# A gated FFT filter and state-space layer on one Trainium2 core: a third buffer for the skip products, and a new order of all five engines

## The chip, the core and the metric

The kernel runs on one NeuronCore of a Trainium2 chip, in one launch. The metric is the device time of one execution in microseconds. Five engines take instructions, each strictly in its own written order: PE (matrix multiplication; its weight loads are shown apart as PEld), DVE (vector), ACT (scalar and activation), POOL, which here mostly issues accumulating DMAs, and SP, which only issues DMAs. They wait for each other through semaphores.

## The reference

`x` is 2048 tokens by 1024 features. Two branches are computed from it and mixed by a gate of one number per token:

```python
g = sigmoid((x * gate_w).sum(-1, keepdims=True))
# A: spectral filter over both axes
a = irfft2(rfft2(x) * (w_r + 1j * w_i))
# B: diagonal complex state-space layer
h[t] = Lam_bar * h[t-1] + B_bar @ x[t]          # 1024 complex states, 2048 steps
b = 2 * (h @ Cmat.T).real + x * Dskip
out = g * a + (1 - g) * b
```

Types in and out are bfloat16.

## The kernel before

Both branches run interleaved from the start to the end, so that PE always has a matmul to do. The work is cut into some 900 pieces, each a generator step of a Python function. The string `ORDER` names one piece per letter, and `PIECES` gives the order of the 169 vector steps of the state-space recurrence (letter `v`). Pieces are issued in that order, and it fixes the order on all five engines; `SLOTS` says which of four PSUM slots (1024 fp32 columns each) each PSUM tile takes. Nothing is rescheduled later, so an instruction that waits holds up everything behind it on its engine.

The stages that the prediction speaks of:

- **Head.** `load_x` brings in `x`; `turn` (L938) transposes it on PE; `turn_out` (L947) and `fold` (L961 to L972) prepare it on DVE; `fd` (L442 to L455) multiplies by the DFT along the features, `fd_out` (L461) moves each result from PSUM on ACT; `s1` (L474) is the first DFT step along the tokens, done as small 64-row matmuls, and `s1_out` (L489) moves it. Between these, ACT and DVE build tables for the recurrence (`sincos`, L1129 to L1136, `make_tab`, L281 to L306). A PSUM slot is free for the next PE piece when its ACT or DVE copy is done.
- **Middle.** `unit_mm` (L410) multiplies `x` by B in eight chunks of 256 tokens, `unit_out` (L420) copies out, and DVE runs the recurrence (L340 to L387) with ACT's help (L372). The spectral branch goes on with `s2` (L609) and `is1` (L648).
- **Output stage.** `early_mm` (L732) multiplies the states by C for ten tiles of 128 tokens, in halves. `scale_y` (L763, ACT) multiplies a half by 1-g into a tile `ye` (two buffers), and `early_store` (L773, SP) stores it in `y_scratch` in DRAM. `mul_skip` (L788, DVE) forms x times Dskip; `scale_skip` (L798, ACT) multiplies a half of it by 1-g into one of two buffers `su`; `add_skip` (L804, POOL) adds the buffer to the stored half in `y_scratch` by an accumulating DMA. So L798 waits until the add of two halves earlier has read its buffer, that is, has landed. Meanwhile `is2` (L681) is the next spectral step, and `is2_out` (L690, ACT) copies its result into `ZT`.
- **End.** `spectral_mm` (L825, L829), `spectral_out` (L836, ACT) and `spectral` (L844 to L865, DVE) finish branch A; `add_late` (L870, POOL) adds `y_scratch` to it, and `close` (L878, SP) stores the tile. Tiles 13 to 15 come last: `own_mm` (L746) fills `ps_q`, `skip_last` (L911, DVE) forms their skip part and `last_out` (L918, DVE) the output.

Of the kernel before, what the change touches and what calls it, by code (L numbers as in the profile page):

```python
# [14 lines left out]
FP32 = mybir.dt.float32  # L15
BF16 = mybir.dt.bfloat16
# [6 lines left out]
K = 512  # L23
H = K // 2
P = 128
# [16 lines left out]
TURN_DVE = tuple(range(16))  # L42
CLOSES = (0, 1, 2, 3, 10, 4, 5, 11, 12, 6, 7, 8, 9)
PIECES = (
# [7 lines left out]
)  # L52
SLOTS = (
    "0123012301230123021302130231023102302302130230123013021302301201320320213023021310102312012301230210",
    "2302021302130230230213132012031203203123120310321032103210130212031203120",
)
MIRROR = (6, 7, 8, 9)
ORDER = (
    "xTxUfTUVfVVa|2xTTGfVVVrrffa|tfUUtGGFFaxEfftffTTxUESbSbtfU2fFTaxAxTffUUfrFAE2fftxSaakFtEAEtfxbbbbbtTT",
    "TFtTbEbUUbFSUUf~ttfFEufSUUU1UbSSArESttfFAAAftFtbbbttEEwttthH~tfthfftufFFSHbtAtttvfvEEtvgvbSASKhtt1r1",  # L60
    "AtAe1vttrtHtr~1vftve111~htuuhttvtFrttF1ttvtHfvthh1vv1tttEttvcEvccccvccctHvSevvSSFcHHwFAAhhEwScKvE11v",
    "KvvSccctttvvtvvAhKvHeevhvcccvv1nAA1KK1swHvvvvvHHsYvvvvkMvvvvssssvhvvvvvHvvnnLYYsvvvvvvnNWssJNsJNNvsh",
    "MhsvsvvJvsvWyHMss344jhvvMM3hHvLvv5vWmm++HnH54v56nMyvvMMWv78378v4nnmmJNvJNvv5hv5vJ56Yvhv4NJyNjYvM+vvM",
    "453WM787HH44y55hH+mm67h8Hv+n7vWm3Nn54JWYvvnvv558468+vvvhMv3vmvJj5NMMv77+8484vYnJN+ydmvyN55JWvvvHhd6h",
    "3H787mM8Hvv555+mjn6M44hYN77vv+5vm3n55HJv644dvyJ8n87N7+Jmv5v5v5vvv+8vh6NnYvym7vv878Hh8qhq+mNviqJivHh+",
    "miiiIqIniv+vHHvIIvvYyivvIJXv+IvvqvYvvnIqviXNvyiJnimqiIinmvYNIiihIIIvvvvvvvJvvNNvq%iiIIIIv++hHHlzlvpp",
    "hvllzZZPZZZZPRRQQRRRmXvHdJhRpzzDmD+ZZRZZHvPZZlJQvoRpOvQvPlDzBzZZovZvOlZpovRYRZlZDzzvvoRRBDoOOvoyQRQB",
    "BlvDDv+POBZOZRBZZvZvlZzzpvZZQDoovvQoDCZYZZooZ9PooYRyRRRDyYRRQQ9CC9000999DDD09000",
)

EVEN = ((0, 0), (2, 1), (2, 0), (0, 1))
# [73 lines left out]
def kernel(  # L145
# [50 lines left out]
    fx = ctx.enter_context(tc.tile_pool(name="fx", bufs=1, side="right"))  # L196
# [8 lines left out]
    def psum(shape, name, dtype=FP32):  # L205
        return ps.tile(shape, dtype, name=name, tag=next(slots, "ps"), bufs=1 if SLOTS else 4)
# [27 lines left out]
    fft = {}  # L234
# [190 lines left out]
                        recur(c, slice(0, 8), lambda c=c: xQ[:, 2 * (c % 2):2 * (c % 2) + 2].rearrange("p e (r j) t -> p e r (j t)", r=2).rearrange("p e r (j t) -> p e r j t", t=TS))  # L425
                    yield

    Acol = fx.tile([P, 2, 16], BF16, name="Acol")
    t1_w = turn1_dram.rearrange("(g j) m k -> j m g k", g=2)
    A1s, X1s, psf, pss = {}, {}, {}, {}  # L430

# [101 lines left out]
    def middle():  # L533
        after_ia()
        yield
        JP_sb, KRS_sb, Wc = fft["JP"], fft["KRS"], fft["Wc"]

        def reverse_m(src_bf, ncol, name):
            rps = psum([P, 16, ncol], name + "_ps")
            nc.tensor.matmul(rps[:, 0, :], lhsT=JP_sb[:, 1, :], rhs=src_bf[:, 0, :], start=True, stop=True)  # L540
            nc.tensor.matmul(rps[:, 1:16, :], lhsT=JP_sb[:, 0, :], rhs=src_bf[:, 15:0:-1, :], start=True, stop=True)
            return rps

        wrps = reverse_m(Wc, 4, "Wrev")
        yield
        Wrev = fx.tile([P, 16, 4], FP32, name="Wrev")
        nc.scalar.copy(out=Wrev, in_=wrps)
        yield
        Wh = fx.tile([P, 16, 4], FP32, name="Wh")
        nc.gpsimd.tensor_add(out=Wh[:, :, 0:4:2], in0=Wc[:, :, 0:4:2], in1=Wrev[:, :, 0:4:2])  # L550
        nc.gpsimd.tensor_sub(out=Wh[:, :, 1:4:2], in0=Wc[:, :, 1:4:2], in1=Wrev[:, :, 1:4:2])
        AB = fx.tile([P, 2, 2, 16], FP32, name="AB")
        Wq = Wh.rearrange("p b (c r) -> p c r b", r=2)
        nc.gpsimd.tensor_add(out=AB[:, 0], in0=Wq[:, 0], in1=Wq[:, 1])
        nc.gpsimd.tensor_sub(out=AB[:, 1], in0=Wq[:, 0], in1=Wq[:, 1])
        nc.gpsimd.tensor_scalar_mul(out=AB, in0=AB, scalar1=0.25)
        yield
        aps = psum([32, P], "aps", BF16)
        nc.tensor.transpose(out=aps, in_=Acol.rearrange("p g j -> p (g j)"), identity=ident)
        yield  # L560
        Bcol = fx.tile([32, 3, 4, 16], BF16, name="Bcol")
        nc.scalar.copy(out=Bcol[:, 0:2], in_=aps.rearrange("j (r b a) -> j r a b", r=2, a=4))
        nc.scalar.activation(out=Bcol[:, 2], in_=Bcol[:, 0], func=ACT.Copy, scale=-1.0)
        yield
        zps = psum([P, 2, 16], "zps")
        Kc_sb, Ks_sb = fft["K3"][:, 0], fft["K3"][:, 1]
        for i in range(8):
            nc.tensor.matmul(zps, lhsT=(Kc_sb, Ks_sb)[i // 4][:, i % 4, :], rhs=Bcol[:, i // 4:i // 4 + 2, i % 4, :],
                             start=(i == 0), stop=(i == 7))
        yield  # L570
        Zp = fx.tile([P, 16, 2], BF16, name="Zp")
        nc.scalar.copy(out=Zp, in_=zps.rearrange("p c b -> p b c"))
        yield
        zrp = reverse_m(Zp, 2, "Zrev")
        yield
        Zr = fx.tile([P, 2, 16], FP32, name="Zr")
        nc.scalar.activation(out=Zr[:, 1], in_=zrp[:, :, 1], func=ACT.Copy, scale=-1.0)
        yield
        Q = fx.tile([P, 2, 2, 2, 16], FP32, name="Q")
        each = lambda t: t.unsqueeze(2).to_broadcast([P, 2, 2, 16])  # L580
        every = lambda t: t.unsqueeze(1).to_broadcast([P, 2, 2, 16])
        nc.scalar.copy(out=Zr[:, 0], in_=zrp[:, :, 0])
        yield
        nc.vector.tensor_mul(out=Q[:, 0], in0=each(AB[:, 0]), in1=every(Zp.rearrange("p b r -> p r b")))
        yield
        nc.vector.tensor_mul(out=Q[:, 1], in0=each(AB[:, 1]), in1=every(Zr))
        nc.vector.tensor_add(out=Q[:, 0], in0=Q[:, 0], in1=Q[:, 1])
        yield
        Qb = fx.tile([P, 16, 2], BF16, name="Qb")
        nc.vector.tensor_sub(out=Qb[:, :, 0], in0=Q[:, 0, 0, 0], in1=Q[:, 0, 1, 1])  # L590
        nc.vector.tensor_add(out=Qb[:, :, 1], in0=Q[:, 0, 1, 0], in1=Q[:, 0, 0, 1])
        yield
        qps = psum([P, 32], "qps")
        nc.tensor.matmul(qps, lhsT=KRS_sb[:, 2, :], rhs=Qb.rearrange("p b r -> p (b r)"), start=True, stop=True)
        yield
        Qn = fft["Qn"] = fx.tile([P, 16, 2], BF16, name="Qn")
        nc.scalar.copy(out=Qn.rearrange("p b r -> p (b r)"), in_=qps)
        yield
# [186 lines left out]
    def mul_skip():  # L785
        for tb in range(16):
            if tb not in DIAG:
                nc.vector.tensor_mul(out=xs[tb], in0=xs[tb], in1=fft["Db"])  # L788
                yield

    xgs = {}

    def scale_skip():
        xg = up.tile([P, 2, 2, K], BF16, name="su")
        for tb in range(NEARLY):
            for hf in range(2):
                xgs[tb, hf] = xg[:, hf].rearrange("p a k -> p (a k)").bitcast(FP32)
                nc.scalar.activation(out=xgs[tb, hf], in_=xs[tb][:, K * hf:K * (hf + 1)], func=ACT.Copy, scale=omg[:, tb:tb + 1])  # L798
                yield

# [237 lines left out]

    gB = cpool.tile([P, 16], FP32, name="gB")
    omg = cpool.tile([P, 16], FP32, name="omg")  # L1040
    fft["JP"] = fx.tile([P, 2, P], BF16, name="JP_sb")
    fft["KRS"] = fx.tile([P, 3, P], BF16, name="KRS_sb")

    def load_turns():
# [140 lines left out]
    def once(f):  # L1185
        f()
        yield
# [8 lines left out]
        "%": once(load_Gi), "Y": load_skip(), "y": mul_skip(), "m": scale_skip(), "+": add_skip(), "d": make_dgD(), "X": turn_own(),  # L1196
        "l": spectral_mm(late_tiles), "z": spectral_out(late_tiles), "Z": spectral(late_tiles), "Q": add_late(), "D": close(),
        "p": spectral_mm(own_tiles), "P": spectral_out(own_tiles), "R": spectral(own_tiles), "o": own_mm(), "O": own_out(), "B": own_add(),
# [40 lines left out]
```

## Time and profile before

| | us |
|---|---|
| median of 3 runs | 301.17 (300.79 to 302.21) |
| profiled execution | 303.33 |
| its span, first to last instruction | 301.6 |
| PE busy | 292.6 |
| DVE busy | 284.2 |
| ACT busy | 209.5 |
| POOL busy | 81.0 |

The span is what the profile's time axis shows; the profiled execution's own time is 1.7 us longer. PE's granted clock is 1.00 of full speed throughout. PE has 2446 matmuls, DVE 359 instructions, ACT 323. In rows of the profile, `x16` counts instructions merged into one row, `<-` leads from what is written to what is read, and a bracket or a trailing `<-` names what ended an engine's idle time.

### The profile page before, as it was taken

The page shows a single profiled execution, that of the slowest core. Times are in us where ns is not written, and L with a number is a line of the kernel's source. Part 1 is how long each engine was busy: PE and PEld are TensorE (multiplying, and loading weights), DVE is VectorE, ACT ScalarE, POOL GpSimd, SP SyncE. Part 2 cuts the span into 40 slices and gives each one's busy share as a digit, 9 for nine tenths or more (in the row PEclk, how much of TensorE's full clock was granted, in tenths as well). Part 3 has the DMA queues.
Part 4 walks back from the last instruction along what each step waited for, and adds up shares of the span by engine and source line. Part 5 has one row for each costly group of instructions (what it writes and reads, how often), then busy time and mean ns, then how long its engine had stood idle before and what let it go on. Part 6 is the DMA issues. An engine that isn't in the chain of part 4 may idle for free. (4 is left out here: it accounts for less than half of the span.)

```text
span 301.6 us, 6230 instructions
## 1 busy us (share of the span) xinstructions
PE 292.6 (97%) x2446; PEld 194.6 (65%) x2446; DVE 284.2 (94%) x359; ACT 209.5 (69%) x323; POOL 81.0 (27%) x107
## 2 busy tenths in 40 slices
PE   7899999999999999999999999999979999999995
PEld 4465868977764874477546754688547996556443
DVE  4999999999889999999988999999997899999994
ACT  1899999998531578757685989757969885267100
POOL 2232276696460020200310111201111042244230
PEclk9999999999999999999999999999999999999999
DMA  6999999999978779878995895878999419999995
GB/s 216 289 281 202 196 159 311 153 142 175 196 213 242 196 181 237 211 217 208 222 275 161 180 256 124 195 229 251 250 225 189 79 19 193 124 184 193 124 163 190
DMA packets 74140, 59.21 MB, mean 196 GB/s; under 512 B 44872, under 2 KB 61664, under 8 KB 74112
## 3 DMA queue, kind: packets, MB, share of 16 engines
q1 hardware_dynamic: 66560, 49.69, 64.8%
q0 software_dynamic: 6896, 8.69, 23.8%
q8 instruction: 19, 0.31, 0.5%
q10 hardware_dynamic: 656, 0.44, 0.5%
q14 instruction: 9, 0.07, 0.1%
HBM read 27.33 MB, written 23.08 MB: 167 GB/s over the span
## 5 line engine op out<-in xcount | busy, mean ns | idle before, releaser
L410 PE MATMUL psu<-xQ,BT 128*128 128x256 bf16 x1024 | 116.2, 273 | 0.0
L410 PEld LDWEIGHTS <-BT 128*128 128x128 bf16 x1024 | 98.9, 98 | 16.9 <-issue 4.2
L732 PE MATMUL ps_y<-CT,h 128*128 128x512 bf16 x416 | 93.6, 380 | 0.7 <-ACT ye L763 0.6
L732 PEld LDWEIGHTS <-h 128*128 128x128 bf16 x416 | 39.8, 98 | 47.9 <-issue 4.0
L804 POOL DMA_DIRECT2D y_scratch<-su x20 | 19.2, 987 | 122.9 <-ACT su L798 84.8
L420 ACT CAST h<-psu 128x1024 bf16<-128x1024 f32 x32 | 32.3, 1013 | 15.3 <-PE psu L410 14.6
L343 DVE TENSOR_TENSOR h<-h,tab 128x4096 bf16<-128x4096 bf16 (+1 forms) x20 | 37.4, 1870 | 0.2
L368 DVE TENSOR_TENSOR_SCAN h<-rz,h 128x512 bf16<-128x512 f32 (+1 forms) x14 | 35.9, 2584 | 0.1
L340 DVE TENSOR_TENSOR xQ<-h,tab 128x4096 bf16<-128x4096 bf16 x12 | 27.4, 2284 | 0.3 <-ACT h L420 0.2
L763 ACT ACTIVATE ye<-ps_y,omg 128x512 f32<-128x512 f32 x26 | 17.2, 682 | 12.3 <-PE ps_y L732 6.1
L372 ACT ACTIVATE xQ<-h,r_sb 128x254 bf16<-128x254 bf16 x48 | 20.5, 508 | 1.4 <-DVE h L368 1.4
L870 POOL DMA_DIRECT2D BT<-y_scratch x10 | 12.7, 1543 | 32.1 <-ACT h L420 16.7
L746 PE MATMUL ps_q<-CT,h 128*128 128x512 bf16 (+2 forms) x112 | 20.9, 349 | 0.0
L836 ACT ACTIVATE BT<-ps_id,gB 128x1024 bf16<-128x1024 f32 x14 | 14.9, 1114 | 6.0 <-DMA out_dram<-BT 6.0
L656 ACT CAST C<-ps_is 128x1024 bf16<-128x1024 f32 x16 | 15.6, 1011 | 4.6 <-PE ps_is L648 3.8
L798 ACT ACTIVATE su<-xs,omg 128x512 f32<-128x512 bf16 x20 | 14.1, 722 | 6.7 <-DVE xs L788 3.0
L619 ACT CAST X<-ps_s 128x1024 bf16<-128x1024 f32 x16 | 16.1, 1008 | 3.8 <-PE ps_s L609 2.6
L690 ACT CAST ZT<-ps_is 128x1024 bf16<-128x1024 f32 x16 | 16.8, 1125 | 0.6 <-ACT su L798 0.6
L746 PEld LDWEIGHTS <-h 128*128 128x128 bf16 x112 | 10.4, 98 | 10.5
L461 ACT CAST X<-ps_fd 128x1024 bf16<-128x1024 f32 x16 | 15.8, 1019 | 0.4 <-PE ps_fd L455 0.4
L289 POOL CAST tab<-sc 128x512 bf16<-128x512 f32 x4 | 4.9, 1234 | 23.3 <-ACT sc L1136 23.3
L947 DVE COPY xQ<-pt 128x1024 bf16<-128x1024 bf16 x12 | 7.8, 683 | 3.5 <-PE pt L938 3.5
(210 smaller groups left out, 440.8 us busy)
## 6 DMA issues: line engine op xcount, KB each, us to landing
y_scratch<-ye SPq DMA_DIRECT2D x20, 256.0 KB, 3.9
y_scratch<-su POOLq DMA_DIRECT2D x20, 256.0 KB, 6.5
Bb<-turn_scratch SPq DMA_DIRECT2D x16, 256.0 KB, 4.9
turn_scratch<-C SPq DMA_DIRECT2D x16, 256.0 KB, 3.4
raw<-turn_scratch SPq DMA_DIRECT2D x8, 512.0 KB, 5.0
xs<-in_A_x_dram SPq DMA_DIRECT2D x13, 256.0 KB, 4.4
out_dram<-BT SPq DMA_DIRECT2D x11, 256.0 KB, 4.5
CT<-in_A_x_dram SPq DMA_DIRECT2D x5, 512.0 KB, 4.7
```

Of the source, the lines that this page charges most:

```text
L340: nc.vector.tensor_mul(out=tmps["s"], in0=u[:, :, ::-1], in1=bc(i))
L343: nc.vector.tensor_mul(out=u, in0=u, in1=bc(i))
L368: nc.vector.tensor_tensor_scan(out=seg, data0=flat(rz, i), data1=seg, initial=0.0, op0=ALU.mult, op1=ALU.add)
L372: nc.scalar.activation(out=tmps["s"][:, 0, :, i, 1:TS], in_=u[:, 1, :, i, 0:TS - 1], func=ACT.Copy, scale=r2_sb[:, js.start + i:js.start + ...
L410: nc.tensor.matmul(psu[:, j, :], lhsT=BT[4 * q + j][:, ri, d8, :], rhs=xQ[:, c, d8, :], start=(d8 == 0), stop=(d8 == 7))
L420: nc.scalar.copy(out=hs[c][:, :, ri, 4 * q:4 * q + 4].rearrange("p e b (q j) -> p e b q j", j=16), in_=psus.pop((c, q, ri)).rearrange("p b ...
L619: nc.scalar.copy(out=X2s[g][:, :, b], in_=ps2s[g][b])
L690: nc.scalar.copy(out=fft["ZT"][:, kp, :, :, 2 * G:2 * G + 2], in_=pszs.pop((G, kp)).rearrange("p v (x n) -> p x n v", n=64))
L732: nc.tensor.matmul(psy, lhsT=hs[c][:, tq, ri, jb, :], rhs=CT[ri][:, jb, 512 * dh:512 * (dh + 1)], start=(i == 0), stop=(i == 15 and tb not ...
L746: nc.tensor.matmul(psq, lhsT=hs[c][:, tq, ri, jb, :], rhs=CT[ri][:, jb, at:at + n], start=(i == 0), stop=(i == 15))
L763: nc.scalar.activation(out=ye, in_=psys[tb][:, K * hf:K * (hf + 1)], func=ACT.Copy, scale=omg[:, tb:tb + 1])
L804: nc.gpsimd.dma_start(out=y_dram[tb, hf], in_=xgs[tb, hf], accum_op=ALU.add)
```

## The change

There are two parts.

First, ten small tiles of the spectral branch's first token column (`Acol`, `Wrev`, `Q` and the like, and the matrix pair `JP`) are no longer tiles of their own; they are cut from one tile `smalls`. All of them are dead when the output stage starts its skip products, and the first 1024 of its 1248 bfloat16 columns then serve `scale_skip` as a third buffer. L798 (now L812) therefore waits for the add of three halves earlier instead of two.

Second, `PIECES`, `SLOTS` and `ORDER` are all new. No piece is added, removed or changed: each engine runs the same instructions of the same shapes in another order (ACT's rows count 257 for 254 and DVE's 341 for 337 only because equal neighbours are merged in the listing).

```diff
-    "miiiIqIniv+vHHvIIvvYyivvIJXv+IvvqvYvvnIqviXNvyiJnimqiIinmvYNIiihIIIvvvvvvvJvvNNvq%iiIIIIv++hHHlzlvpp",
+    "IvvmvvJvvv+HiiHvvvvIIIynqvviiiniinIvvvYyqiqviiqIInNN+I%mIIiIIJvvJvvvivvvhvvNINJ+vviIIHvvhvlHzlzmvvZZ",
...
-    Acol = fx.tile([P, 2, 16], BF16, name="Acol")
+    smalls = fx.tile([P, 1248], BF16, name="smalls")
+    small_at = [0]
+
+    def small_tile(rows, shape, dtype):
+        n = int(np.prod(shape)) * (2 if dtype == FP32 else 1)
+        at = small_at[0]
+        small_at[0] += n + n % 2
+        assert small_at[0] <= 1248
+        v = smalls[0:rows, at:at + n]
+        v = v.bitcast(FP32) if dtype == FP32 else v
+        names = "abcd"[:len(shape)]
+        return v.rearrange("p (%s) -> p %s" % (" ".join(names), " ".join(names)), **dict(zip(names, shape))) if len(shape) > 1 else v
+
+    Acol = small_tile(P, [2, 16], BF16)
...
-        Wrev = fx.tile([P, 16, 4], FP32, name="Wrev")
+        Wrev = small_tile(P, [16, 4], FP32)
...
         xg = up.tile([P, 2, 2, K], BF16, name="su")
         for tb in range(NEARLY):
             for hf in range(2):
-                xgs[tb, hf] = xg[:, hf].rearrange("p a k -> p (a k)").bitcast(FP32)
+                at = (2 * tb + hf) % 3
+                xgs[tb, hf] = xg[:, at].rearrange("p a k -> p (a k)").bitcast(FP32) if at < 2 else smalls[:, 0:2 * K].bitcast(FP32)
                 nc.scalar.activation(out=xgs[tb, hf], in_=xs[tb][:, K * hf:K * (hf + 1)], func=ACT.Copy, scale=omg[:, tb:tb + 1])
...
-    fft["JP"] = fx.tile([P, 2, P], BF16, name="JP_sb")
+    fft["JP"] = small_tile(P, [2, P], BF16)
```

Three places show how the order moves. Line numbers of the changed kernel are 13 to 14 higher from L429 on; L372, L383, L387 and L343 keep theirs.

ACT in the output stage, before: `ZT` rows are the copies of `is2` (two instructions of a row are one copy), `ye` rows the scaling of C's output, `su` rows the skip products, `xQ` rows the help for the recurrence.

```order
215 L690 CAST ZT<-ps_is_3037 128x512x2
216 L763 ACTIVATE ye<-ps_y,omg 128x512
217 L798 ACTIVATE su<-xs,omg 128x512
218 L690 CAST ZT<-ps_is_3085 128x512x2
219 L798 ACTIVATE su<-xs,omg 128x512
220 L763 ACTIVATE ye<-ps_y,omg 128x512
221 L690 CAST ZT<-ps_is_3099 128x512x2
222 L690 CAST ZT<-ps_is_3126 128x512x2
```

The same place now:

```order
222 L703 CAST ZT<-ps_is_3046 128x512x2
223 L776 ACTIVATE ye<-ps_y,omg 128x512 x2
224 L703 CAST ZT<-ps_is_3071 128x512x2
225 L812 ACTIVATE su<-xs,omg 128x512
226 L703 CAST ZT<-ps_is_3080 128x512x2
227 L703 CAST ZT<-ps_is_3116 128x512x2
228 L703 CAST ZT<-ps_is_3127 128x512x2
229 L703 CAST ZT<-ps_is_3136 128x512x2
```

Before, the skip products of tile 8 (rows 217 and 219, halves 16 and 17 counted from 0) stood around the two scalings. Now the two scalings stand together, half 16 follows one copy later, and half 17 comes only after the first two copies of `spectral_out`.

ACT in the head, before: `X` rows are the copies of `fd`, L1122 and L1123 turn two vectors, L281 makes the angles, the others are sine and cosine.

```order
10 L1114 ACTIVATE rinv_156<-are 128x8
11 L1122 CAST vecF<-vps 128x8
12 L1123 COPY gw_150<-vps 128x256
13 L281 ACTIVATE ang<-tau_f,ang_153 128x256 x2
14 L1133 ACTIVATE a_kk<-ang_153 128x16
15 L1134 ACT_TABLE_LOAD
16 L1134 ACTIVATE SC<-ang_153 128x16
17 L461 CAST X_285<-ps_fd 128x1024
18 L461 CAST X_318<-ps_fd 128x1024
```

The same place now:

```order
10 L1128 ACTIVATE rinv_155<-are 128x8
11 L281 ACTIVATE ang<-tau_f,ang_152 128x256
12 L1147 ACTIVATE a_kk<-ang_152 128x16
13 L1148 ACT_TABLE_LOAD
14 L1148 ACTIVATE SC<-ang_152 128x16
15 L1150 ACTIVATE SC<-a_kk,chpi 128x16
16 L1136 CAST vecF<-vps 128x8
17 L1137 COPY gw_149<-vps 128x256
18 L281 ACTIVATE ang<-tau_f,ang_152 128x256
19 L474 CAST X_310<-ps_fd 128x1024
20 L474 CAST X_312<-ps_fd 128x1024
```

The two vector copies and one small cosine now stand between the table load and the first copy of `fd`; one of the two angle rows went the same way.

DVE near the end, before: L343, L387 and L383 are the last steps of the recurrence's last chunk, L844 and L846 belong to branch A, L911 is the skip part of tile 13.

```order
312 L343 TENSOR_TENSOR h<-h,tab 128x4096
313 L844 TENSOR_TENSOR BT<-BT 128x2x2x128
314 L846 TENSOR_TENSOR BT<-BT 128x2x2x128
315 L387 TENSOR_TENSOR h<-h,xQ 128x2x1024
316 L383 TENSOR_TENSOR h<-h,xQ 128x2x1024
317 L911 SCALAR_TENSOR_TENSOR xQ<-xs,omg,BT 128x1024
```

The same place now:

```order
315 L925 SCALAR_TENSOR_TENSOR xQ<-xs,omg,BT 128x1024
316 L343 TENSOR_TENSOR h<-h,tab 128x4096
317 L858 TENSOR_TENSOR BT<-BT 128x2x2x128
318 L387 TENSOR_TENSOR h<-h,xQ 128x2x1024
319 L860 TENSOR_TENSOR BT<-BT 128x2x2x128
320 L383 TENSOR_TENSOR h<-h,xQ 128x2x1024
```

The skip part of tile 13 moved ahead of the recurrence's last steps.

On PE the head changes too: before, after the sixth `turn` piece came two `s1` pieces and then the third `fd` piece; now the third and fourth `fd` pieces come directly after the sixth `turn` piece. Over the whole head the sixteen 64-row `s1` pieces stood in seven runs of neighbours and now stand in nine. On SP, the stores of halves 16 and 17 of `y_scratch` (L773, halves counted from 0) stood between the loads of the last `is2` inputs, that of half 18 after the load of the last constant `Gi` (L714) and that of half 19 two closing stores later. Now all four follow the last `is2` inputs and `Gi`, whose issue waits for the `is2` pieces of group 5.

More of the change, by code (lines that the diff above doesn't have):

```diff
@@ L44 @@
 PIECES = (
[7 rows of a table removed]
[7 rows of a table added]
 )
 SLOTS = (
-    "0123012301230123021302130231023102302302130230123013021302301201320320213023021310102312012301230210",
-    "2302021302130230230213132012031203203123120310321032103210130212031203120",
+    "0123012312031203120310231021302130213021302132012031203120120320132032020123123012312012031203121031",
+    "0231230132013213213210102132103210210321321302310231201302102312031232013",
 )
@@ L58 @@
 ORDER = (
[L59 to L65, printed above, removed]
-    "miiiIqIniv+vHHvIIvvYyivvIJXv+IvvqvYvvnIqviXNvyiJnimqiIinmvYNIiihIIIvvvvvvvJvvNNvq%iiIIIIv++hHHlzlvpp",
-    "hvllzZZPZZZZPRRQQRRRmXvHdJhRpzzDmD+ZZRZZHvPZZlJQvoRpOvQvPlDzBzZZovZvOlZpovRYRZlZDzzvvoRRBDoOOvoyQRQB",
-    "BlvDDv+POBZOZRBZZvZvlZzzpvZZQDoovvQoDCZYZZooZ9PooYRyRRRDyYRRQQ9CC9000999DDD09000",
+    "xTUffxTUV2VffVVVVaxG|TTGGFfataa|tfxxUUFTffafffTEEttxttFfFUrrEETTTbUatfkfUUSSAAtUfxtTT2StAUrffxUttxFF",
+    "f2TSEwSbFbbffU~fuUUtrFEUUAAbbtfEttSSEAAFEfFtEbbbbSAtthHttttfff~u~bfbbhHbFFuF1ttbtrtSvtEtEvKgthtEebtt",
+    "1vv11fvtf111ttt~hh1vA1tfeccvHcttttvtthhHtvvwvcSSttcSvvvvtttttHHHuvFFAvvcrcAArEEvvehcSrvvwc1vS1cc1AAt",
+    "ttvFEvthvcvvvvScvcHvAS1Avcch1ee1vvvvKKKkvvvvv1hhKKvsHHHvvvvvYYhHYwsMvsLvssvsvvnnnNNWvvvsvMvsvMvyJJvn",
+    "vvWsssssHvvhMsNJhvHvNsWW3jvvMm+s44JHh3vjv5HmM4Lvnym5v54vvnNMYJ+67878mM+Nn53v4vnyvY55v4JWvN6m57NJm8yW",
+    "+7hHhHJM3455M+vv8hvv46vhvjHvmmHn+MM5377NvvJ545vn46v88vvYNn577dvyM3M44v5XM8J5vvnNN67hHM87hh+vHvv+vmm+",
+    "W3vWvH885jv55+vn6YYyv445myh737JN885mYvv5Hnv4vJJ645vn+d7785mm5dh8NvvN67878+nHhXHhJyvNmvvq+ivqqiqYhIJi",
+    "IvvmvvJvvv+HiiHvvvvIIIynqvviiiniinIvvvYyqiqviiqIInNN+I%mIIiIIJvvJvvvivvvhvvNINJ+vviIIHvvhvlHzlzmvvZZ",
+    "ZpZmZl++pPhZPQzJlphRRzvRXRRpHHZZPQRYyoDPZlllZdODoozRzo+lvZoZQlmQDDvROovvZZzvZZvBBRRZlzZQoOORvRvvvZZQ",
+    "pRBZZvDDvRZovZOBOv+zBCDzBvZYDpvZvQZZZZYDPPR9oYRo0ooyRRRRDC990QQQDD090yC90Y9o9D00",
 )
@@ L545, in middle @@
         yield
-        Wrev = fx.tile([P, 16, 4], FP32, name="Wrev")
+        Wrev = small_tile(P, [16, 4], FP32)
         nc.scalar.copy(out=Wrev, in_=wrps)
         yield
-        Wh = fx.tile([P, 16, 4], FP32, name="Wh")
+        Wh = small_tile(P, [16, 4], FP32)
         nc.gpsimd.tensor_add(out=Wh[:, :, 0:4:2], in0=Wc[:, :, 0:4:2], in1=Wrev[:, :, 0:4:2])
         nc.gpsimd.tensor_sub(out=Wh[:, :, 1:4:2], in0=Wc[:, :, 1:4:2], in1=Wrev[:, :, 1:4:2])
-        AB = fx.tile([P, 2, 2, 16], FP32, name="AB")
+        AB = small_tile(P, [2, 2, 16], FP32)
         Wq = Wh.rearrange("p b (c r) -> p c r b", r=2)
@@ L560, in middle @@
         yield
-        Bcol = fx.tile([32, 3, 4, 16], BF16, name="Bcol")
+        Bcol = small_tile(32, [3, 4, 16], BF16)
         nc.scalar.copy(out=Bcol[:, 0:2], in_=aps.rearrange("j (r b a) -> j r a b", r=2, a=4))
@@ L570, in middle @@
         yield
-        Zp = fx.tile([P, 16, 2], BF16, name="Zp")
+        Zp = small_tile(P, [16, 2], BF16)
         nc.scalar.copy(out=Zp, in_=zps.rearrange("p c b -> p b c"))
@@ L575, in middle @@
         yield
-        Zr = fx.tile([P, 2, 16], FP32, name="Zr")
+        Zr = small_tile(P, [2, 16], FP32)
         nc.scalar.activation(out=Zr[:, 1], in_=zrp[:, :, 1], func=ACT.Copy, scale=-1.0)
         yield
-        Q = fx.tile([P, 2, 2, 2, 16], FP32, name="Q")
+        Q = small_tile(P, [2, 2, 2, 16], FP32)
         each = lambda t: t.unsqueeze(2).to_broadcast([P, 2, 2, 16])
@@ L588, in middle @@
         yield
-        Qb = fx.tile([P, 16, 2], BF16, name="Qb")
+        Qb = small_tile(P, [16, 2], BF16)
         nc.vector.tensor_sub(out=Qb[:, :, 0], in0=Q[:, 0, 0, 0], in1=Q[:, 0, 1, 1])
```

14 rows, old and new, of the table PIECES are left out of this document.

## Prediction

> **What bounds the kernel now.** I read the head of the page first, then the waits of PE, then the chain that ended last, then timelines around its steps. The page, busy time and count of each engine:
>
> ```profile
> span 301.6 us, 6230 instructions
> PE 292.6 (97%) x2446; PEld 194.6 (65%) x2446; DVE 284.2 (94%) x359; ACT 209.5 (69%) x323; POOL 81.0 (27%) x107
> ```
>
> PE is the bound: it lacks 9.0 us of being busy for the whole span, and DVE is close behind with 17.4 us free. A new order takes no work from either, so it can win at most what PE spends waiting, and can lose wherever a wait appears. The waits of PE (us in total, times, longest):
>
> ```profile
> PE ps_is L681 <- ACT ye L763: 1.3, 1, 1.3
> PE ps_fd L455 <- DMA G_sb<-c_G: 1.2, 2, 1.0
> PE psw L1005 <- DVE A L1000: 1.2, 1, 1.2
> PE ps_y L732 <- ACT ye L763: 0.6, 1, 0.6
> PE pt L938 <- DMA CT<-in_A_x_dram: 0.5, 1, 0.5
> PE ps_is L681 <- ACT ZT L690: 0.4, 1, 0.4
> PE ps_fd L442 <- ACT CT L489: 0.2, 1, 0.2
> PE ps_y L732 <- ACT X L619: 0.2, 1, 0.2
> ```
>
> Together 5.6 us. Three of these are the start (the constant `G`, `A`, the first `x`: 2.9 us), which the change doesn't touch. The rest is 2.7 us, and 1.7 of it lies at one place, which the chain shows (start, duration, what):
>
> ```profile
> 205.78 1.45 SPq L782
> 207.27 6.59 DMA y_scratch<-ye
> ...
> 214.40 8.28 DMA y_scratch<-su
> 222.77 0.72 ACT su L798
> ...
> 225.10 0.61 PE ps_is L681 x8
> ...
> 264.62 3.45 PE ps_y L732 x16
> ...
> 277.63 20.77 PE ps_q L746 x112
> ```
>
> The store of half 15 takes 6.59 us, the add of half 15 then 8.28 us, and only then may ACT write half 17 into the same `su` buffer; the scaling `ye` and the `is2` copy stand behind it, and PE behind these. From 225.10 on the chain is PE's own work. ACT's and PE's timelines there (the bracket is the idle time before, and what ended it):
>
> ```profile
> 222.77 0.72 ACT L798 ACTIVATE su<-xs,omg 128x512 f32<-128x512 bf16 x1 [2.42 <-DMA y_scratch<-su]
> ...
> 224.11 0.61 PE L681 MATMUL ps_is<-KRS_sb,raw 128*128 128x128 bf16 x8 [1.30 <-ACT ye L763]
> 225.10 0.61 PE L681 MATMUL ps_is<-KRS_sb,raw 128*128 128x128 bf16 x8 [0.38 <-ACT ZT L690]
> ```
>
> **The change part by part.** *The third buffer, and half 17 placed later.* The 2.42 us wait of ACT goes: half 17 now asks for the add of half 14, issued a half earlier, and stands behind two `spectral_out` copies besides. PE's 1.30 + 0.38 us go with it. ACT's rows behind it need PE's output only, and half 16 waits for half 13. So −1.7.
>
> How long an add takes in general stands in the profile's list of transfers (KB each, median us from issue to landing):
>
> ```profile
> y_scratch<-ye SPq DMA_DIRECT2D x20, 256.0 KB, 3.9
> y_scratch<-su POOLq DMA_DIRECT2D x20, 256.0 KB, 6.5
> ```
>
> So 6.5 us, and 8.28 in the chain; ACT came to half 17 at 222.77 − 2.42 = 220.35. A rule speaks against this term: the Trainium skill, "DMA: Bandwidth & Descriptors", section "Anatomy of one DMA — SWDGE (gpsimd) path", fits a GpSimd DMA by about 2.0 us and the bytes over 436 GB/s; my estimate from that page is 2.6 us for 256 KB. By it the add would be down at 217.0, the wait would not be there and this term would be nothing; the trace disagrees by a factor of 2.5 to 3.2, and the trace decides here.
>
> *The short waits in the middle.* PE's 0.6 and 0.2 us for `ye` and `X` (fourth and last row of the waits) are gone in the new order, by what stands ahead of the pieces. But other pieces now come as near to their releasers: `unit_mm` piece 8 to the copy of `s1` piece 12, piece 21 to the scaling of half 11, whose store now queues behind others, `early_mm` 18 to the `is2` copy of group 7. Counting the durations of what stands between, I find some 0.35 us of room at each. I give back what is won: 0, with −0.8 and +1.0 as the ends (all won; two of the three fail by half a `ye`).
>
> *The head, on ACT.* The timeline of ACT, 6 to 18 us:
>
> ```profile
> 8.06 0.14 ACT L1122 CAST vecF<-vps 128x8 f32<-128x8 bf16 x1
> 8.11 0.37 ACT L1123 COPY gw<-vps 128x256 bf16<-128x256 bf16 x1
> 9.27 0.91 ACT L281 ACTIVATE ang<-tau_f,ang 128x256 f32<-128x256 f32 x2 [0.79 <-DVE ang L1131]
> ...
> 10.30 1.28 ACT L1134 ACT_TABLE_LOAD   x1
> ...
> 11.72 1.91 ACT L461 CAST X<-ps_fd 128x1024 bf16<-128x1024 f32 x2
> ...
> 14.56 0.30 ACT L1136 ACTIVATE SC<-a_kk,chpi 128x16 f32<-128x16 f32 x1
> ```
>
> L1122 and L1123 took from 8.06 to 8.48 and were followed by 0.79 us of idleness: they were free. Now these 0.42 us and the 0.30 of L1136 stand after the 9.27, which waits for DVE as before, and ahead of the first `fd` copy. That copy started at 11.72 and takes 1.91 / 2 = 0.96, so it ended at 12.7; now 13.4. PE there:
>
> ```profile
> 12.05 1.06 PE L938 MATMUL pt<-ident_g,CT 128*128 128x128 bf16 x16
> 13.04 1.24 PE L474 MATMUL ps_s<-X,raw 64*128 64x512 bf16 x8
> 14.21 0.61 PE L445 MATMUL ps_fd<-G_sb,preT 128*128 128x256 bf16 x4
> ...
> 15.53 0.67 PE L938 MATMUL pt<-ident_g,CT 128*128 128x128 bf16 x9
> ```
>
> Before, two `s1` pieces (13.04 to 14.21) stood between the sixth `turn` piece, which ends at 13.0, and the third `fd` piece, which needs the slot that the first copy frees. Now `fd` follows directly at 13.0 and waits till 13.4: +0.4. The first `s1` piece, after three more `turn` pieces, waits for the fourth `fd` copy: the two `fd` pieces end at 13.4 + 2 × 1.32 (14.21 to 15.53) = 16.0, its copy at 17.0, PE's three `turn` pieces (0.5 each, 1.06 / 2) at 17.5. That has 0.5 us of room, which a further delay on DVE eats; I count 0 to +0.45 there and 0 to +0.25 for the fifth `fd` piece behind its DVE fold. DVE moves two table steps ahead of the last `turn_out` copies (up to +0.4). I take +0.9, with +0.3 and +1.5 as the ends: some of it is only a shift of PE's order, but nothing after it gives time back, as PE is busy from there on.
>
> *The `s1` pieces in nine runs for seven.* A single piece and a run of four:
>
> ```profile
> 24.46 0.60 PE L474 MATMUL ps_s<-X,raw 64*128 64x512 bf16 x4
> ...
> 26.62 1.90 PE L474 MATMUL ps_s<-X,raw 64*128 64x512 bf16 x16
> ```
>
> In a run a piece takes 1.90 / 4 = 0.48, alone 0.60 and the next row starts 0.53 later. Entering and leaving the 64-row shape thus costs 0.05 to 0.2, and there are two more of it: +0.3 (0.1 to 0.4).
>
> *The end, on DVE.* The last recurrence step, and the skip part of tile 13 that moved ahead of it:
>
> ```profile
> 281.69 1.22 DVE L383 TENSOR_TENSOR h<-h,xQ 128x2048 bf16<-128x2048 bf16 x1
> 282.82 1.28 DVE L911 SCALAR_TENSOR_TENSOR xQ<-xs,omg,BT 128x1024 f32<-128x1024 bf16 x1
> ```
>
> The recurrence's end moves from 282.9 to about 284.2. The first `own_mm` matmul that needs it comes after 32 matmuls of tile 13 from 277.63, at 20.77 / 112 = 0.185 each on average and 0.216 at full width (3.45 / 16 in the chain's `ps_y` rows), so between 283.6 and 284.5. By the width of these matmuls, which is the full one, I take the later: 0.3 us of room, so 0, up to +1.0 if another 0.7 us of DVE slips.
>
> *The tiles in `smalls`.* Reads and writes keep their shapes; in the program's order their last reader stands ahead of the first skip product on the third buffer. 0.
>
> Sum: −1.7 + 0 + 0.9 + 0.3 + 0 + 0 = −0.5 against the profiled execution's 303.33, so 302.8 there. The profiled execution lies 2.2 us above the median of 301.17; I carry the difference over: **300.7**. Its ends, with each term at a likely rather than its extreme end, are 299.6 and 301.8. About 0.5%, or 1.5 us, is what a measurement of this kernel can tell from no change.
>
> **The rivals.** *Nothing is given back* (faster). The head is only two rows in another order, and the ends of its term begin at +0.3; if the waits for the slots fall within copies that overlap, and the middle keeps its −0.8, the sum is −1.7 − 0.8 + 0.3 = −2.2: 299.0. For it: PE's short waits stand in the profile and are gone in the new order. Against: 0.42 us of free ACT work now lies behind a table load.
>
> *The stores of halves 16 and 17 come too late* (slower). SP now issues them only after `Gi`, which waits for `is2` piece 11 on PE. Half 18's scaling on ACT needs the buffer that half 16's store reads. From the end of piece 11, PE has piece 12, `early_mm` 19, two `is2` pieces, a `unit_mm` and an `is2` piece, and then a `unit_mm` that needs the slot of the scaling of half 19. The groups' rows and the store's landing time:
>
> ```profile
> L410 PE MATMUL psu<-xQ,BT 128*128 128x256 bf16 x1024 | 116.2, 273 | 0.0
> L763 ACT ACTIVATE ye<-ps_y,omg 128x512 f32<-128x512 f32 x26 | 17.2, 682 | 12.3 <-PE ps_y L732 6.1
> L690 ACT CAST ZT<-ps_is 128x1024 bf16<-128x1024 f32 x16 | 16.8, 1125 | 0.6 <-ACT su L798 0.6
> ```
>
> PE: 0.45 + 3.45 + 0.9 + 3.6 (116.2 / 32 pieces) + 0.45 = 8.9 us, an `is2` piece taken as 0.45 since two merged ones of the chain's kind take about 0.9. ACT: scaling 0.68, copy 1.13, scaling 0.68, and SP's issue of the load and the store 0.7, together 3.2. So a landing above 5.7 us decides. The median is 3.9, but the store in the chain took 6.59, when SP, as here, had issued loads right before it. If it took as long as the add's 8.28, PE would wait 2.6 us: 303.3. For it: four stores now go out together. Against: the median.
>
> *The stall is not in the timed executions.* They are 2.2 us shorter than the profiled one. An add that landed in the page's median, 6.5 us, would end at 214.40 + 6.5 = 220.9, not 222.7, and PE would have waited for next to nothing. Then the first term is 0, the sum +1.2: 302.4. The chain's 8.28 us speak against it. By the page of the Trainium skill named above such short landings would be the rule.
>
> *The change doesn't do what it says.* If the third buffer shares its releases with the old small tiles' readers, L798 waits as before; the new order alone has moved half 17 away, and the time stays near 301.2.
>
> **How the numbers follow.** Forecast, 299.6 to 301.8: 0.38. Nothing given back, 299.0: 0.34. Stores too late, 303.3: 0.15. No stall in the timed executions, 302.4: 0.10. No third buffer, 301.2: 0.03. The range 298.4 to 303.2 takes in the first two, the last two and the smaller half of the late stores. Faster than 299.7 are most of the second case and a little of the first: 0.33. Slower than 302.7 are most of the third and a part of the fourth: 0.16. The rest is 0.51.
>
> **What would show it.** Right: no wait of ACT for `y_scratch<-su` above 1 us near 222, no wait of PE for `ye` before `is2`, and about 1 us more of PE idleness between 13 and 22 us than before. Wrong: PE's first `s1` rows at the same time as before after equal work (then the second case), a wait of PE for `ye` ahead of the `unit_mm` before the last `spectral_mm` stage (the third), a gap of PE before 285 us ahead of `own_mm` (the end's term), or a wait in the middle above 1 us that I have put at nothing.

## The result, and the profile after

The changed kernel takes 303.59 us (median of 8 runs, 303.40 to 303.89), the kernel before, beside it, 301.29 us (8 runs, 300.65 to 303.04). The ratio is 1.0068, with a 95% interval of 1.0043 to 1.0093: slower by 0.4 to 0.9%. The forecast was 300.7 us, and 303.59 lies above its range.

The profiled execution of the changed kernel took 303.89 us, with a span of 302.1 us. The head of its page:

```profile
span 302.1 us, 6208 instructions
...
PE 292.4 (97%) x2427; PEld 195.2 (65%) x2446; DVE 285.6 (95%) x359; ACT 209.7 (69%) x323; POOL 75.5 (25%) x107
```

Nineteen matmul records are missing here (2427 against 2446 weight loads), so PE's counts are not compared. The waits of PE:

```profile
PE psw L1019 <- DVE A L1014: 1.2, 1, 1.2
PE ps_fd L468 <- DMA G_sb<-c_G: 1.2, 1, 1.2
PE psu L410 <- ACT A_last L502: 1.1, 1, 1.1
PE ps_s L487 <- DVE xQ L961: 0.7, 1, 0.7
PE ps_s L487 <- ACT X L474: 0.3, 1, 0.3
PE ps_is L694 <- DMA raw<-turn_scratch: 0.3, 1, 0.3
PE ps_y L745 <- ACT ye L776: 0.2, 1, 0.2
```

The waits of `is2` for `ye` and `ZT` are gone, as forecast. ACT's timeline there shows half 16 (L812) without any wait for an add, and half 17 no longer between the copies:

```profile
221.51 1.29 ACT L776 ACTIVATE ye<-ps_y,omg 128x512 f32<-128x512 f32 x2
222.66 1.13 ACT L703 CAST ZT<-ps_is 128x1024 bf16<-128x1024 f32 x1
223.62 0.77 ACT L812 ACTIVATE su<-xs,omg 128x512 f32<-128x512 bf16 x1
224.24 1.13 ACT L703 CAST ZT<-ps_is 128x1024 bf16<-128x1024 f32 x1
```

New are waits in the head (0.7 and 0.3), one of 0.3 us for a load of the output stage (`raw`), and one of 1.1 us for a copy of `s1`, the longest that the order makes. PE in the head, and at that place:

```profile
13.07 0.60 PE L458 MATMUL ps_fd<-G_sb,preT 128*128 128x256 bf16 x4 [0.21 <-DVE rot_kk L1143]
...
17.47 0.61 PE L487 MATMUL ps_s<-X,raw 64*128 64x512 bf16 x4 [0.30 <-ACT X L474]
18.78 0.61 PE L487 MATMUL ps_s<-X,raw 64*128 64x512 bf16 x4 [0.70 <-DVE xQ L961]
...
72.07 3.65 PE L410 MATMUL psu<-xQ,BT 128*128 128x256 bf16 x32 [1.06 <-ACT A_last L502]
```

The last row is `unit_mm` piece 8. Its slot is the one that `s1` piece 12 filled, so it has to wait until ACT has copied that piece. ACT there:

```profile
65.97 1.98 ACT L474 CAST X<-ps_fd 128x1024 bf16<-128x1024 f32 x2
69.43 1.70 ACT L372 ACTIVATE su<-h,r_sb 128x254 bf16<-128x254 bf16 x4 [1.48 <-DVE h L368]
71.03 1.90 ACT L502 CAST A_last<-ps_s 128x1024 bf16<-128x1024 f32 x2
```

ACT has nothing to do for 1.48 us, since its next instruction, the recurrence help L372, waits for DVE's scan; the copy stands behind. Before, the copy that PE needs stood first of the three lines:

```profile
64.59 1.03 ACT L489 CAST A_last<-ps_s 128x1024 bf16<-128x1024 f32 x1
65.49 1.96 ACT L461 CAST X<-ps_fd 128x1024 bf16<-128x1024 f32 x2
68.30 1.70 ACT L372 ACTIVATE su<-h,r_sb 128x254 bf16<-128x254 bf16 x4 [0.85 <-DVE h L368]
```

The copy (`A_last` at 64.59) ran while DVE was still at work, and PE went through. So the profile has a stall of 1.7 us less and about 2 us of new waits more, and its span (302.1) is 0.5 us above that of the first profile of before (301.6). The medians are 2.3 us apart. The profiled execution of before had been 2.2 us above its median, that of the changed kernel is 0.3 us above its own. What the first profile shows at 222 us might thus not be what most executions do.

Theory A: the stall of before at the `is2` pieces is an accident of some executions, its removal is worth nothing in the median, and the new waits ahead of 85 us are the whole loss. Theory B: the stall is always there, and the loss has arisen in the output stage or beyond.

### The profile page after: what moved, and what is told of

Read it like the earlier page. It is cut to its first block, busy times and chain, and to the rows that moved or that the text cites. A ratio compares the mean times of both kernels' runs of the same rounds, so it can differ in the third digit from the quotient of the medians.

```text
span 302.1 us, 6208 instructions
## 1 busy us (share of the span) xinstructions
PE 292.4 (97%) x2427; PEld 195.2 (65%) x2446; DVE 285.6 (95%) x359; ACT 209.7 (69%) x323; POOL 75.5 (25%) x107
## 4 chain that ended last, share of the span: by engine, by line
PE 72%; DVE 19%; DMA 3%; ACT 2%; POOL 1%; issue 1%; SPq 0%; DVEq 0%; ACTq 0%
PE ps_y L745 30%; PE psu L410 26%; PE ps_q L759 7%; DVE xQ L961 3%; PE ps_is L694 2%; PE ps_id L843 2%; DMA raw<-turn_scratch 2%; DVE sums L977 2%; DVE preT L975 2%; DVE h L368 2%; PE ps_is L661 2%; DVE tab L306 1%; PE ps_s L622 1%; PE ps_id L839 1%; DVE preT L980 1%
## 5 line engine op out<-in xcount | busy, mean ns | idle before, releaser
L410 PEld LDWEIGHTS <-BT 128*128 128x128 bf16 x1024 | 99.3, 98 | 16.9 <-issue 5.0
L745 PE MATMUL ps_y<-CT,h 128*128 128x512 bf16 x401 | 92.5, 379 | 1.1 <-ACT ye L776 0.2
L343 DVE TENSOR_TENSOR h<-h,tab 128x4096 bf16<-128x4096 bf16 (+1 forms) x20 | 37.3, 1865 | 0.3
L818 POOL DMA_DIRECT2D y_scratch<-su x14 | 14.6, 1058 | 73.6 <-ACT su L812 44.2
L372 ACT ACTIVATE xQ<-h,r_sb 128x254 bf16<-128x254 bf16 x48 | 20.8, 503 | 0.1
L818 POOL DMA_DIRECT2D y_scratch<-smalls x6 | 5.2, 864 | 57.8 <-ACT smalls L812 39.8
L289 POOL CAST tab<-sc 128x512 bf16<-128x512 f32 x4 | 4.1, 1020 | 28.4 <-ACT sc L1150 28.4
```

Of the source, the lines that this page charges most:

```text
L343: nc.vector.tensor_mul(out=u, in0=u, in1=bc(i))
L372: nc.scalar.activation(out=tmps["s"][:, 0, :, i, 1:TS], in_=u[:, 1, :, i, 0:TS - 1], func=ACT.Copy, scale=r2_sb[:, js.start + i:js.start + ...
L410: nc.tensor.matmul(psu[:, j, :], lhsT=BT[4 * q + j][:, ri, d8, :], rhs=xQ[:, c, d8, :], start=(d8 == 0), stop=(d8 == 7))
L745: nc.tensor.matmul(psy, lhsT=hs[c][:, tq, ri, jb, :], rhs=CT[ri][:, jb, 512 * dh:512 * (dh + 1)], start=(i == 0), stop=(i == 15 and tb not ...
L818: nc.gpsimd.dma_start(out=y_dram[tb, hf], in_=xgs[tb, hf], accum_op=ALU.add)
```

## The experiments

Each kernel was timed beside the kernel before, in three series, in which the median of before was 300.67 to 300.84 us (301.29 beside the changed kernel); the differences are at the end of this section. Two versions of one series are compared more firmly than two of different ones.

**The kernel before once more.** No edit.

> The kernel before, unchanged, to see a second profile of it and its spread. Theory A (the wait of ACT for the add of half 15 near 220 us is not there in most executions, so its removal is worth little in the median): an execution near 301 us shows less than 0.5 us of that wait and less than 0.5 us of idleness of PE at the is2 pieces near 222 to 225 us; one near 303 us shows about 2.4 and 1.7 us. Theory B (the wait is always there, and the 303.33 of the first profiled execution came from elsewhere): about 2.4 and 1.7 us whatever the time of the execution.

Its median is 300.96 us (12 runs, 300.40 to 302.06), its profiled execution took 301.09. ACT's rows for halves 16 and 17, and POOL's for the adds of halves 14 and 15:

```profile
218.49 0.71 ACT L798 ACTIVATE su<-xs,omg 128x512 f32<-128x512 bf16 x1
219.10 1.09 ACT L690 CAST ZT<-ps_is 128x1024 bf16<-128x1024 f32 x1
220.08 0.72 ACT L798 ACTIVATE su<-xs,omg 128x512 f32<-128x512 bf16 x1
220.69 0.68 ACT L763 ACTIVATE ye<-ps_y,omg 128x512 f32<-128x512 f32 x1
```

```profile
207.34 0.86 POOL L804 DMA_DIRECT2D y_scratch<-su  x1 [13.52 <-ACT ZT L690]
211.36 0.86 POOL L804 DMA_DIRECT2D y_scratch<-su  x1 [3.16 <-DMA y_scratch<-ye]
```

Half 17 follows without a wait. The store of half 15 came down earlier, so its add went out at 211.36, not at 214.40 as in the first profile, and had landed before ACT came to the buffer. PE's list of waits has no row for `is2`. What the stall costs can be read from PE's rows on both sides of it, in the first profile:

```profile
218.75 3.62 PE L732 MATMUL ps_y<-CT,h 128*128 128x512 bf16 x16
...
225.54 3.62 PE L732 MATMUL ps_y<-CT,h 128*128 128x512 bf16 x16
```

and in this one:

```profile
218.60 3.62 PE L732 MATMUL ps_y<-CT,h 128*128 128x512 bf16 x16
222.05 1.50 PE L681 MATMUL ps_is<-KRS_sb,raw 128*128 128x128 bf16 x24
223.39 3.62 PE L732 MATMUL ps_y<-CT,h 128*128 128x512 bf16 x16
```

From one `L732` row to the next it is 6.79 us there and 4.79 here. So the stall cost 2.0 us, nearly all of the 2.2 us between the two executions. The same kernel has executions with the stall (303.33) and without it (301.09), and the median, 300.96, is that of the latter: theory A.

**The first 85 us of before, the rest changed.** Of the changed order the first 345 pieces are taken and laid among themselves as before, each in the slot it had before:

```python
first = set(new[:345])                       # pieces as (letter, number)
order = [p for p in old if p in first] + new[345:]
```

> As before, but with the first 345 of the 980 pieces (about the first 85 us) in the order and the slots of before. Theory A: the wait at 72 us goes too, so 2.0 to 2.6 us faster than the changed kernel, about 301.2, as fast as before. Theory B: no change, 303.6.

300.97 us, a ratio to before of 1.0005 (0.9996 to 1.0013). The whole loss is gone, though the third buffer and the new order of output stage and end are in. Its waits of PE behind the start are 0.2 us each:

```profile
PE ps_y L746 <- ACT ye L777: 0.2, 1, 0.2
PE ps_fd L456 <- ACT CT L503: 0.2, 1, 0.2
PE psu L411 <- ACT h L421: 0.2, 1, 0.2
```

Theory B falls. Where ahead of 85 us the loss lies, the next runs tell.

**The first 35 us alone.** The same with 160 pieces for 345.

> The changed kernel, but the first 160 of its 980 pieces (about the first 35 us) stand among themselves in the order, and in the PSUM slots, that they have before; everything behind is the changed order. Theory A (the loss is in PE's waits of the head and at 72 us): the 1.0 us more of waits before 35 us and most of the 0.5 us of more entries into small matmul shapes go, the 1.06 us at 72 us stays: 1.0 to 1.5 us faster than the changed kernel, about 302.3. Theory B (the loss is in the output stage, the third buffer or its order): no change, 303.6.

307.21 us, 6.5 us above before where the changed kernel is 2.3 above: the expectation failed, by a wait that the mixture itself makes. The row of PE's waits, and PE's row behind that wait:

```profile
PE psu L411 <- ACT CT L503: 3.6, 1, 3.6
...
39.07 5.28 PE L411 MATMUL psu<-xQ,BT 128*128 128x256 bf16 x32 [3.65 <-ACT CT L503]
```

At the seam (the place where the two orders meet) the copy of `s1` piece 7 stands, as before, behind a row of table steps on ACT, while the changed order has a `unit_mm` that needs its slot at once. The cost is larger than the wait: right behind it PE's granted clock was 0.50 from 39 to 42 us, and the 32 matmuls took 5.28 us, where the changed kernel's at 72.07 took 3.65. It says nothing on the head, but shows what such a misplaced copy costs. A seam ahead of that copy does better:

**The first 27 us.** The same with 142 pieces.

> The changed kernel, with only its first 142 of 980 pieces (about the first 27 us) in the order and the PSUM slots of before, so that ACT's copy of s1 piece 7 keeps its changed place. Theory A (loss in the head's waits, then at 72 us): the 1.0 us of waits at 13 to 21 us goes, but DVE is the engine whose lateness makes the wait at 72 us, and it is only about 1.1 us late there because of the head: 1.0 to 2.0 us faster than the changed kernel, 301.6 to 302.6. Theory B (the head's waits are made good later anyway): no change, 303.3 to 303.6.

302.58 us, 1.9 us above before: 0.4 us won against the changed kernel by these differences, less than the 1.0 to 2.0 expected. The head's waits of 0.70 for DVE and for the slot of `fd` are gone; 0.6 us is lost anew at this seam, for a copy of `s1` as well, where before lost 0.2. So the head is worth some 0.8 us. The wait at 72 us stays:

```profile
PE psu L411 <- ACT A_last L503: 0.9, 1, 0.9
```

**One copy ahead of the recurrence help.** In the changed order, piece 12 of `s1_out` (the first `A` of the two) moves to directly behind its matmuls (a part of one line of `ORDER`):

```diff
-Srvvwc1vS1cc1AA
+SArvvwc1vS1cc1A
```

> The changed kernel with one piece moved: ACT's copy of s1 piece 12 now stands ahead of the recurrence help of L372, not behind it. Theory A: PE no longer waits 1.06 us at 72 us for that copy; the recurrence step behind comes up to 1.2 us later on DVE, which has some room there; 0.5 to 1.1 us faster than the changed kernel, 302.5 to 303.1. Theory B (a wait of PE there is made good later, since DVE's recurrence bounds the middle): no change, or slower by the 1.2 us that DVE loses.

303.22 us, 2.5 us above before: nothing won that can be told from the spread. The wait at 72 us is gone, and one of the same length stands at 87:

```profile
86.92 1.25 PE L411 MATMUL psu<-xQ,BT 128*128 128x256 bf16 x10 [1.00 <-ACT h L421]
```

ACT shows why:

```profile
72.00 0.99 ACT L503 CAST A_last<-ps_s 128x1024 bf16<-128x1024 f32 x1
...
84.27 1.70 ACT L373 ACTIVATE su<-h,r_sb 128x254 bf16<-128x254 bf16 x4 [5.75 <-DVE h L369]
85.88 3.72 ACT L421 CAST h<-psu 128x1024 bf16<-128x1024 f32 x4
```

The next help instruction waits for DVE, which is about 1.1 us later now because the first help came later; ACT is idle for 5.75 us, and four copies of `unit_mm` stand behind it, two of them of pieces that PE had finished long before. As it stands this speaks for theory B's reading of the place (DVE bounds it). The next run decides.

**These copies ahead of the help too.** Besides the edit above, the copies of `unit_mm` 8 and 9, with the four pieces that they need (a store, two small copies, the start of the middle stage), move ahead of the second help (again a part of a line):

```diff
-vvvvv1hhKKvsHHH
+vv1KKsHHvvvhhvH
```

> The changed kernel with the copy of s1 piece 12 ahead of the recurrence help L372 (as in the run with that one move), and the copies of unit_mm pieces 8 and 9 also ahead of the next recurrence help, so that neither of them stands behind ACT's wait for DVE's scan. Theory A (PE's waits at 72 and 87 us come from copies queued on ACT behind a help instruction that waits for DVE): both waits go and nothing takes their place, 0.9 to 1.3 us faster than the changed kernel, about 302.2. Theory B (DVE itself bounds this stretch): the wait shows up once more further on, no change, 303.2.

302.06 us, 1.4 us above before: 0.9 us won against the changed kernel, as theory A had it. The firmer comparison is inside this series of runs: the changed kernel with two buffers (below), with the same 1.1 us wait at 72 us, took 303.21 to 304.00 us there, this one 301.90 to 302.51, so 1.2 us less in the median. Behind 30 us PE has one wait left:

```profile
PE ps_y L746 <- ACT ye L777: 0.2, 1, 0.2
```

DVE's next scan ends as late as in the run before (the help starts at 84.24 us against 84.27); it is not DVE that held PE up, but copies queued behind an ACT instruction that waits for DVE.

**Both.** The 142 pieces as before, and the copies moved.

> Both edits together: the first 142 pieces in the order of before, and the copies on ACT ahead of the recurrence help as in a12h. Theory A: both losses go, about 301.0, equal to before within 0.3 us. Theory B: at least 302.

301.57 us, ratio 1.0025 (1.0010 to 1.0039), 0.9 us above before. The two gains add up (0.4 + 0.9 of 2.3; against the two-buffer kernel of the same series 0.7 and 1.2, together 1.7), but before isn't reached, so neither expectation holds. Of the rest the profile shows 0.4 us, the seam's wait (0.61 against 0.18 in before):

```profile
28.58 0.38 PE L456 MATMUL ps_fd<-G_sb,preT 128*128 128x128 bf16 x2 [0.61 <-ACT CT L503]
```

Another 0.3 to 0.5 us, which the run with 345 pieces wins back, stays open. The small matmul shapes don't explain it: in PE's traces the `s1` pieces stand in eight runs before and with 345 pieces, and in nine here and in the changed kernel. That is one run more, not two as was said ahead of the prediction, and by the prediction's own rows it costs 0.05 to 0.2 us.

**Two buffers in the changed order.** `% 3` becomes `% 2`. In this kernel some of the skip products are overwritten before they are added, since the changed order issues products up to two halves ahead of the add.

> The changed kernel with two buffers for the skip products instead of three, all else kept. If the third buffer is what takes away ACT's waits for the adds: one or more waits of L812 for an add above 1 us come back in the output stage, and 0.5 to 2 us on the time. If the new order alone does it, or there was nothing to take away in most executions: the same time as the changed kernel within 0.3 us, 303.6.

303.29 us, 2.6 us above before, against 2.3 for the changed kernel. ACT waits once for an add, by 0.6 us:

```profile
ACT su L813 <- DMA y_scratch<-su: 0.6, 1, 0.6
```

PE doesn't wait for it. The changed order needs the third buffer to be right. That it isn't needed to be fast is shown only for the waits that are left here: an add that is issued behind the product that overwrites its buffer holds nothing up, as it would have to in a right kernel with two.

**The third buffer alone.** The kernel before with its own order, and the first part of the change.

> The kernel before, in its own order and slots, with the third buffer alone (the small tiles cut from one, and the skip products taking turns over three buffers). Theory A (the wait for the add of half 15 occurs only in some executions): the median stays within 0.3 us of before, 300.7, no execution shows a wait of ACT for an add above 0.3 us at half 17, and the slow tail of the times of before (302 to 303) is missing. Theory B (that wait costs every execution 1.7 us): 1.5 us faster than before, 299.2. Theory C (the shared small tiles bring waits of their own): slower than before by over 0.5 us, with waits for smalls in the profile.

300.77 us, ratio 0.9991 (0.9957 to 1.0025): no gain in the median. Long executions are not gone either, against the expectation: times go up to 304.75, those of before beside it to 305.24. The profiled execution is such a one, with a span of 303.0 us, and shows another accident, in the waits and in PE's rows:

```profile
PE ps_y L746 <- DMA CT<-in_B_C_re_dram: 1.4, 1, 1.4
...
PE ps_y L746 <- DMA CT<-in_B_C_im_dram: 0.6, 1, 0.6
...
90.74 8.54 PE L746 MATMUL ps_y<-CT,h 128*128 128x512 bf16 x31 [0.62 <-DMA CT<-in_B_C_im_dram]
```

Two loads of C's matrix came late at 90 us; at half 17 there is no wait. The second profile of before has, at the same place,

```profile
88.04 7.07 PE L732 MATMUL ps_y<-CT,h 128*128 128x512 bf16 x32
```

and ends these matmuls at 95.1 us where the other ends them at 99.3, 4.2 us later. Of that 0.2 us lies ahead of this place and 2.0 us are the waits. The rest is in the matmuls themselves, and there the granted clock, 1.00 at 88 us in both profiles, was 0.50 here from 91.5 to 94.5 us and 1.00 again from 95 on; in the second profile of before it stayed at 1.00.

**Half 17 later, with two buffers.** The kernel before with `m` of half 17 and `Y` of a later load moved (a part of a line of `ORDER`):

```diff
-nmvYNIiihIIIvvvvvvvJvvNNvq%ii
+nvNIiihIIImvvvvvvvJvvNNvq%Yii
```

> The kernel before with two buffers, but with the skip product of half 17 moved on ACT behind the scaling of half 17 and four is2 copies (and the load of a later skip tile moved behind Gi, since it has to wait for that product). The order alone then takes the wait for the add off PE's path. Theory A: median as before, 300.7 within 0.3 us, without the slow tail. Theory B: 1.5 us faster.

301.32 us, ratio 1.0010 (0.9990 to 1.0030). No gain: half 17 waits 0.4 us for an add at its new place, and PE as long behind it (`psu` for `ZT`, 0.4 us). None of the 12 times is above 301.96, where 4 of the 29 of before beside it are above 302; so few runs don't show that the long executions are gone.

**The first 200 us of before, output stage and end changed.** As with 345 pieces, with 691.

> The changed kernel with its first 691 of 980 pieces (about 200 us) in the order and the slots of before; only the output stage and the end, with the third buffer, are in the changed order. Theory A (all of the loss lies ahead of 85 us, and the rest of the change is worth nothing in the median): 300.7 to 301.0, equal to before and to the run with the first 345 pieces. Rival (the changed output stage gains, and the changed middle hides it in that run): 0.5 to 1.5 us faster than before, about 299.7.

301.25 us, ratio 1.0006 (0.9981 to 1.0032): the changed output stage and end are worth nothing that this interval (0.6 us faster to 1.0 us slower) would show. No version was faster than before by more than the interval.

Median minus that of before measured beside it, us, and its 95% interval from the ratio. The changed kernel's own +2.3 is among the least certain, since the 8 runs of before beside it lie between 300.65 and 303.04:

| kernel | us | 95% |
|---|---|---|
| changed | +2.3 | 1.3 to 2.8 |
| changed, copy of `s1` 12 moved | +2.5 | 1.9 to 2.7 |
| changed, two buffers | +2.6 | 1.6 to 3.2 |
| changed, first 142 pieces as before | +1.9 | 1.1 to 2.1 |
| changed, copies ahead of both helps | +1.4 | 0.7 to 1.7 |
| both | +0.9 | 0.3 to 1.2 |
| changed, first 160 pieces as before | +6.5 | 6.1 to 7.1 |
| changed, first 345 pieces as before | +0.2 | −0.1 to 0.4 |
| changed, first 691 pieces as before | +0.4 | −0.6 to 1.0 |
| before, third buffer alone | −0.1 | −1.3 to 0.8 |
| before, half 17 later | +0.5 | −0.3 to 0.9 |
| before, again | +0.2 | −0.2 to 0.5 |

## Why the prediction was wrong

*The carried difference.* The step that failed first is "The profiled execution lies 2.2 us above the median of 301.17; I carry the difference over". The 1.7 us of the first term are part of that difference: the second profile of before, 2.2 us shorter, lacks the stall, and PE's rows put 2.0 of the 2.2 us there. So the mechanism was read rightly from the trace, and in the changed kernel half 17 stands at 241.52 us, clear of it, but the median never paid for it. Taking the 1.7 us off a median that was 2.2 us lower already took them off twice. The rival "the stall is not in the timed executions" had this, with a chance of 0.10 and 302.4 us. The argument that the chain's 8.28 us speak against it was no argument, as the 8.28 us came from the same execution as the stall.

*The short waits in the middle, taken at 0 with +1.0 as the upper end.* Here the place was named (`unit_mm` 8 behind the copy of `s1` 12) and the size was off. I counted 0.35 us of room from the durations of before; PE waited 1.06 us, which is the last of the signs of being wrong that I had named. That the copy now stands behind an instruction that waits for DVE should have been priced from DVE's side: ACT's idle 0.85 us ahead of L372 in before was the warning, since whatever stands behind L372 starts with the scan's end. It cost 0.9 us by the differences to before, or 1.2 us inside one series, as the run with the copies moved shows.

*The head, +0.9.* The size was about right: PE is idle for 1.4 us between 12 and 22 us in the changed kernel, against 0.2 us in the first and 0.9 us in the second profile of before, and laying the head as before won 0.4 us beside a new loss of 0.4. The place was not: the slot of the third `fd` piece, which I gave +0.4, cost 0.21 us, and the second `s1` piece waits 0.70 us for a slot that a DVE copy frees, which I had only under DVE's slip.

*The small matmul shapes, +0.3.* The count was wrong: nine runs of `s1` pieces against eight, so one more and not two, which by the same rows is 0.05 to 0.2 us. Its time was not measured apart.

*The end, 0; the late stores, a rival with 0.15.* Both as forecast: PE has no wait behind 240 us, none for `ye` ahead of the last `unit_mm` pieces, and the changed tail costs nothing.

With the first term at 0, the middle at +0.9 and one run of small shapes in place of two (+0.1), the prediction's own sum is 0 + 0.9 + 0.9 + 0.1 = +1.9 us: 303.1, against 303.59 measured. That is a check of its terms and not a forecast, since the middle's 0.9 is itself taken from the runs.

## What to carry to other kernels

A stall that a DMA's landing ends is worth little in the median when most executions don't have it: where the profiled execution is well above the median, take a second profile before pricing anything on it. And in a kernel whose engines run in a fixed order, an instruction that waits for a busy engine holds up the copies queued behind it; when a new order puts a slot-freeing copy behind such an instruction, price it from the awaited engine's finish, and when undoing it, move every copy that stands behind the next such wait too.

## What was not expected of the hardware

The same store (half 15 into `y_scratch`, 256 KB) let its add go out at 214.40 us in one profile and at 211.36 in another of the same kernel, where the add ahead of it had been issued at 207.28 and 207.34. Of these 3 us, 1.2 come from SP, which issued the store at 207.27 in one and at 206.10 in the other, because the load ahead of it took SP 1.45 us in place of 0.43. Most of the rest is the transfer, 6.59 us in the one and at most 5.26 in the other. The add itself then took 8.28 us to land in the one and 6.6 in the other. Together that is larger than everything the change could win, the 2.7 us of waits behind the start.

A wait of PE can cost more than its length. Behind the two waits of 2.0 us together at 90 us, and behind that of 3.65 us at 39 us, the granted clock fell to 0.50 for about 3 us; behind the 1.30 us of the stall in the first profile it stayed at 1.00.
